# A conditioned transformer block on one core: the opening's loads and steps in another order, and the last token tile finished in two halves

## The chip, the core and the metric

The kernel runs on one core of a Trainium2 chip. The metric is the device time of one execution in microseconds (us), the median of several runs. Engines are named as in the profile: PE is TensorE's matmul side and PEld its weight loads, DVE is VectorE, ACT is ScalarE, POOL is GpSimd, SP is SyncE, which here only issues DMAs. L338 is line 338 of the kernel before.

## The reference, cut to what matters

One sequence of S = 2048 tokens with D = 576 features, 32 heads of 18, and a hidden width of 4608, all in bfloat16:

```
sa, ca, ga, sb, cb, gb = split(silu(c) @ w_mod, 6)        # six rows of 576
h  = layernorm(x) * (1 + ca) + sa
q, k, v = split(h @ wqkv)                                 # 32 heads of 18
logits[s, w] = q[s] . k[s - 2*w] * 18**-0.5,  w = 0..7    # a window of 8 keys, every second token
o  = sum over w of softmax(logits)[s, w] * v[s - 2*w]
x  = x + ga * (o @ wo)
h  = layernorm(x) * (1 + cb) + sb
out = x + gb * (((h @ w_gate) * (h @ w_up)) @ w_down)
```

Keys before the first token are masked with -1e9.

## The kernel before, in words

**Tiles.** Attention goes by chunks of 256 tokens, each two tiles of 128 (index j is the tile in the chunk). 576 features are five tiles of the contraction (kt), the last of 64 rows. The gated part goes by five groups of token tiles, GROUPS (L40): 2, 4, 4, 3 and 3 tiles. Each group has a gate stage (gate_up, L613 to L662) and a down stage (down, L675 to L718). The gate stage runs over 36 slices of 128 hidden columns, and for each makes a gate bank pg and an up bank pu in PSUM (L621), which ACT casts to u_sb and g_sb (L645, L646) and DVE multiplies into hh (L650). The gate and up weights come in nine blocks of four slices (512 columns, two DMAs of 512 KB on SP's queue, L149), the down weights in nine blocks of 576 KB on POOL's queue (L164).

**Order.** The program order of every engine is written out by hand (L63), and each engine works through its own list in that order. Inside the stages of gate and down, pieces of the attention of later chunks are spread evenly between the matmuls (spread, L603; the tables gbg and dbg, L893 and L914). Before the first gate stage there is an **opening** (L729 to L881) which does the whole attention of chunk 0 and the query, key and value products of chunks 1 and 2. Its steps, in the order of before:

- LayerNorm of chunk 0, tile by tile (ln_parts, L225), the transposes of the result (transposed, L263, whose eviction applies the modulation) into hT, and the first modulation columns (mod_columns, L278, from weights wmA).
- a_qj (L353): the products pq = wqk x hT of chunk 0 (L338), 15 matmuls for a group of up to four 128-column tiles and one token tile, six calls, 90 matmuls; a_ln(1) on DVE stands ahead of them.
- pj (L758): DVE products of queries with keys shifted by the window offset w. lj (L763): PE sums them per head into the bank lgj (L769), the mask first (L767). max_j and sum_j are the softmax (L772, L781).
- a_v (L359): values, PE products pv and pvr (L364, L366), ACT casts to v_sb (L368, L369), POOL DMA to a DRAM tile vd. For chunk 0 the cast stays on the chip as o_sb.
- a_norm, a_t and a_q (L311, L325, L348): the same LayerNorm, transposes and query and key products for chunks 1 and 2, in whole chunks.
- to_keys (L475): PE shifts the softmax weights to the key rows (pk), ACT casts them (keyed). av_mul (L492): DVE weights the values (vsh). av_sum (L499): PE shifts and sums them into three banks po of their own pool, pop, and ACT copies these to oT (L510 to L512).
- mod_row (L290): the row ga as a broadcast. b_wj (L514): the output product pwj (L521), two halves of 288 columns in banks of the common pool; DVE adds to x (L527, L528) and takes the statistics of the second LayerNorm.
- transposed again, to h2T, the input of the first gate stage.
- b_ld (L377): a POOL DMA of 1152 KB that gathers the shifted values of one tile of chunk 1 from vd into vsh. The helper behind (L788) makes this DMA wait until a given weight DMA has landed.

**Queues.** Everything that SP issues is one DMA queue in the order of the text: x of chunk 0, wmA (two pairs of 576 and 72 KB), x of chunk 1 (288 KB), wv (576 and 72 KB), wqk in three pairs (576 and 72, 64 and 8, 512 and 64 KB, L195 to L197), then x of chunk 2, wmB, wo, the weights of mod_row, the residual rows, and the first five blocks of gate and up weights (L804).

**PSUM.** There are eight banks. In the opening five belong to psp0 (all products) and three to pop (po). At the end of the opening both pools are closed and one pool psp of eight banks is opened (L88, L882 to L884).

**The end.** The last group holds three token tiles. Its down stage keeps a bank acc of 512 columns for each tile and one bank accr with the last 64 columns of all (L680, L681). After the first 32 hidden slices, the last four are done by tile: accr of all three, then acc of each (L702 to L711). DVE multiplies by gb (L707, L712) and, after all three tiles have been multiplied, adds to x (L715, L716); SP stores each tile in one DMA (L717).

Of the kernel before, what the change touches and what calls it, by code (L numbers as in the profile page):

```python
# [8 lines left out]
F32 = mybir.dt.float32  # L9
ALU = mybir.AluOpType  # L10
# [8 lines left out]
P = 128  # L19
# [24 lines left out]
def kernel(  # L44
# [40 lines left out]
    wdp = pool("wdp", 3)  # L85
    gup = pool("gup", 3)
    outr = pool("outr", 1)
    guards = [tc.tile_pool(name="psp0", bufs=5, space=PSUM), tc.tile_pool(name="pop", bufs=3, space=PSUM)]  # L88
    psp, pop = [g.__enter__() for g in guards]

    def ps(shape, dt, name):
        return psp.tile(shape, dt, name=name, tag="bank")

    def js(j):
        return slice(j * P, (j + 1) * P)
# [34 lines left out]
    def load_x(i):  # L130
        if i < NCH:
            x_in[i] = sp.tile([P, ST, D], BF, name="x_t1") if i == 1 else xin.tile([P, ST, D], BF, name="x_t")
            nc.sync.dma_start(x_in[i][:], x_rows(i))
# [32 lines left out]
    def load_k(dst, wsrc, c0, n):  # L166
        r = nc.sync.dma_start(dst(slice(0, P), slice(0, KF)), wsrc[0:KF * P, c0:c0 + n].rearrange("(k p) n -> p k n", p=P))
        nc.sync.dma_start(dst(slice(0, 64), KF), wsrc[KF * P:D, c0:c0 + n])
        return r
# [20 lines left out]
    nc.gpsimd.memset(wmCr[64:, :], 0.0)  # L190
    load_wm(wmA, 0, 0)
    load_wm(wmA, 1, 1)
    load_x(1)
    load_k(lambda p, k: wv[p, k, :], A_wqkv, 2 * D, D)
    load_k(lambda p, k: wqk[p, k, 0:D], A_wqkv, 0, D)  # L195
    load_k(lambda p, k: wqk[p, k, D:DP], A_wqkv, 2 * D - 64, 64)
    load_k(lambda p, k: wqk[p, k, DP:2 * D], A_wqkv, D, D - 64)  # L197


    nc.gpsimd.memset(ident[:], 0.0)  # L200
# [105 lines left out]
    def a_ln(i):  # L306
        x = x_in.pop(i)
        xn, rsq, norm = layernorm(lambda j: x[:, j, :], "a")
        aa[i] = dict(xn=xn, rsq=rsq, norm=norm)

    def a_norm(i):  # L311
        aa[i]["rsq"]()
        aa[i]["norm"]()
# [11 lines left out]
    def a_t(i, on_dve=True):  # L325
        a_tiles(i)
        hT = aa[i]["hT"]
        transposed(aa[i]["xn"], lambda m: hT[:, m, :], (0, 1), 0)(on_dve)
# [19 lines left out]
    def a_q(i, g):  # L348
        qk_tiles(i, QGRP[g], slice(0, CH), nc.scalar.copy)
        if g == 2:  # L350
            a_halo(i)

    def a_qj(j, g, evict):  # L353
        qk_tiles(0, QGRPJ[g], js(j), evict)
# [4 lines left out]
    def a_v(i, j):  # L359
        hT = aa[i]["hT"]  # L360
        pv = ps([P, VA * DH], F32, "pv")
        pvr = ps([P, VR * DH], F32, "pvr")
        for kt in range(KT):
            nc.tensor.matmul(pv[:], lhsT=hT[:, kt, js(j)], rhs=wv[:, kt, 0:VA * DH], start=(kt == 0), stop=(kt == KT - 1))  # L364
        for kt in range(KT):
            nc.tensor.matmul(pvr[:], lhsT=hT[:, kt, js(j)], rhs=wv[:, kt, VA * DH:D], start=(kt == 0), stop=(kt == KT - 1))  # L366
        v_sb = vstage.tile([P, DH, H], BF, name="v_sb")[:] if i else v0(j)
        nc.scalar.copy(v_sb[:, :, 0:VA], pv[:].rearrange("p (h d) -> p d h", d=DH))  # L368
        nc.scalar.copy(v_sb[:, :, VA:H], pvr[:].rearrange("p (h d) -> p d h", d=DH))  # L369
        r0 = HALO + i * CH + j * P  # L370
        if i == 0:
            if j == 1:
                nc.gpsimd.dma_start(vd[r0 + P - HALO:r0 + P, :], o_sbs[0][P - HALO:P, j, 0:D])
            return
        nc.gpsimd.dma_start(vd[r0:r0 + P, :], v_sb.rearrange("p d h -> p (d h)"))
# [299 lines left out]
    def down(gi, hh, bg):  # L675
        t0, t1 = GROUPS[gi]
        nj = t1 - t0
        last = FT - FB
        at = spread([(1.0, p) for p in bg], last)
        acc = [ps([P, 512], F32, "acc") for _ in range(nj)]  # L680
        accr = ps([P, 2 * ST, 64], F32, "accr")  # L681

        def mm_a(f, j):
            wb = wd_blk[gi * NBLK + f // FB]
            nc.tensor.matmul(acc[j][:], lhsT=hh[:, f, js(j)], rhs=wb[:, f % FB, 0:512],  # L685
                             start=(f == 0), stop=(f == FT - 1))

        def mm_r(f, j):
            wb = wd_blk[gi * NBLK + f // FB]
            nc.tensor.matmul(accr[:, j, :], lhsT=hh[:, f, js(j)], rhs=wb[:, f % FB, 512:D],  # L690
                             start=(f == 0 and j == 0), stop=(f == FT - 1), skip_group_check=True)

        for f in range(last):
            for j in range(nj):
                mm_a(f, j)
                mm_r(f, j)
            if f % FB == FB - 1:
                load_wd(gi * NBLK + f // FB + 3)
            for piece in at[f]:
                piece()  # L700
        xs = [x1[t // ST][t % ST] for t in range(t0, t1)]
        for j in range(nj):  # L702
            for f in range(last, FT):
                mm_r(f, j)
        o_ts = [gup.tile([P, 512], BF, name="o_t", tag="g_sb" if j % 2 else "u_sb") for j in range(nj)]
        t_r = outr.tile([P, 2 * ST, 64], BF, name="t_r")
        nc.vector.tensor_tensor(t_r[:, 0:nj, :], accr[:, 0:nj, :],  # L707
                                gb_bc[:, None, 512:D].to_broadcast([P, nj, 64]), ALU.mult)
        for j in range(nj):
            for f in range(last, FT):  # L710
                mm_a(f, j)  # L711
            nc.vector.tensor_tensor(o_ts[j][:], acc[j][:], gb_bc[:, 0:512], ALU.mult)  # L712
        for j in range(nj):
            r0 = (t0 + j) * P
            nc.vector.tensor_tensor(xs[j][:, 0:512], o_ts[j][:], xs[j][:, 0:512], ALU.add)  # L715
            nc.vector.tensor_tensor(xs[j][:, 512:D], t_r[:, j, :], xs[j][:, 512:D], ALU.add)  # L716
            nc.sync.dma_start(out_flat[r0:r0 + P, :], xs[j][:])  # L717
        load_wd(gi * NBLK + NBLK + 2)  # L718
# [28 lines left out]
    mod_columns(wmA, 0)  # L747
    for e in ev:
        e()
    a_ln(1)  # L750
    for j in range(ST):
        for g in range(3):
            a_qj(j, g, nc.scalar.copy)

    prods, lgs = {}, {}
    dd0 = smp.tile([P, ST, W, H], F32, name="dd")
# [1 line left out]
    def pj(j, w):  # L758
        off = HALO - DIL * (W - 1 - w) + j * P
        prods[j, w] = prodp.tile([P, KT, P], BF, name="prodj", tag="prod")  # L760
        nc.vector.tensor_tensor(prods[j, w][:], aa[0]["qT"][:, :, js(j)], aa[0]["kT"][:, :, off:off + P], ALU.mult)

    def lj(j, w):  # L763
        if w == 0:
            lgs[j] = ps([P, W, H], F32, "lgj")
            if j == 0:
                nc.tensor.matmul(lgs[j][:], lhsT=ident[:], rhs=maskneg[:], start=True, stop=False, skip_group_check=True)  # L767
        for m in range(KT):
            nc.tensor.matmul(lgs[j][:, w, :], lhsT=prods[j, w][:, m, :], rhs=ind[:, m, :],  # L769
                             start=(m == 0 and j == 1), stop=(m == KT - 1), skip_group_check=True)  # L770
# [17 lines left out]
    def behind(dma, load):  # L788
        tc.add_manual_dep(dma.ins, load.ins.name, SYNC, reason="value rows go first")
# [14 lines left out]
    for g in range(5):  # L804
        load_wgu(g)

    for w in range(2):
        pj(0, w)
    a_norm(1)
    for w in range(2, 4):  # L810
        pj(0, w)
    for w in range(4):
        lj(0, w)
        pj(0, w + 4)
    a_v(0, 0)
    for w in range(4, 8):
        lj(0, w)
    a_v(0, 1)
    for w in range(2):
        pj(1, w)  # L820
    max_j(0)
    for w in range(2, 4):
        pj(1, w)
    a_t(1, False)
    for w in range(4):
        lj(1, w)
    for w in range(4, 6):
# [1 line left out]
    sum_j(0)  # L829
    for w in range(6, 8):  # L830
        pj(1, w)
    a_q(1, 0)
    a_q(1, 1)
    for w in range(4, 8):
        lj(1, w)
    max_j(1)
    mod_columns(wmB, 1)
    a_q(1, 2)
    sum_j(1)
    a_q(1, 3)  # L840
    for j in range(ST):
        to_keys(j)
    av_mul(0, 0)
    a_q(1, 4)
    a_v(1, 0)
    av_mul(0, 1)
    av_sum(0, 0)
    a_v(1, 1)
    a_ln(2)
    aa[2]["rsq"]()  # L850
    av_sum(0, 1)
    av_mul(1, 0)
    aa[2]["norm"]()
    mod_row(lambda p, k: wmC[p, k, :] if k < KF else wmCr[p, :], ga_bc, sc_bc)
    x1_half = b_wj(0)
    av_sum(1, 0)
    av_mul(1, 1)
    a_t(2, False)
    xn2, stat2, rsq2, norm2 = ln_parts(lambda j: x1[0][j], "b")
    x1_half(stat2)  # L860
    rsq2(slice(0, 1))
    av_sum(1, 1)
    a_q(2, 0)
    x1_half = b_wj(1)
    behind(b_ld(1, 0), wgu_in[0])
    behind(b_ld(1, 1), wgu_in[1])
    x1_half(stat2)
    rsq2(slice(1, 2))
    norm2(0)
    ht, _ = h2_of(0)  # L870
    a_q(2, 1)
    transposed(xn2, lambda m: ht[:, m, js(0)], (0,), 2)()
    norm2(1)
    a_q(2, 2)
    a_q(2, 3)
    transposed(xn2, lambda m: ht[:, m, js(1)], (1,), 2)()
    a_q(2, 4)
    for j in range(ST):
        a_v(2, j)
    load_res(1)  # L880
    load_x(4)  # L881
    for guard in [sp_guard] + guards[::-1]:  # L882
# [73 lines left out]
```

## Time and profile before

| What | Value |
|---|---|
| Runs | 575.89 us median (574.8, 575.89, 576.01) |
| The profiled execution | 575.69 us, of which its span is 573.7 us; mean granted clock 0.995 |
| PE busy | 547.6 us, 95% of the span, 5959 matmuls |
| PEld busy | 321.0 us, 56% |
| DVE busy | 327.1 us, 57%, 787 instructions |
| ACT busy | 250.9 us, 44%, 576 instructions |
| POOL busy | 67.2 us, 12%, 103 instructions |
| DMA | 108.13 MB, 188 GB/s on average |
| First matmul of the first gate stage | 63.06 us from the span's start |

A row of a group reads: line, engine, operation, output and inputs by the program's names, shape and number; behind the bar the busy time and the mean of one in ns; then the engine's idle time just before, and what ended it. A row of waits reads: engine, what it ran next, what it waited for, and then the sum in us, the number of times and the longest. A row of the timeline reads: start and busy time in us, engine, line, operation, and in brackets the idle time before it and its releaser. A row of windows reads: the stretch, its length, then busy time and number of instructions of PE, PEld, DVE, ACT and POOL, then the granted clock of PE (1.00 is full), the share of the DMA engines and what they moved in GB/s.

### The profile page before, as it was taken

To read this page: it belongs to the slowest core of one execution; us is meant where nothing else is said; L and a number is where in the kernel's file an instruction comes from. 1 tells how busy PE (TensorE), PEld (TensorE's weight loads), DVE (VectorE), ACT (ScalarE), POOL (GpSimd) and SP (SyncE) were. 2 spreads that over 40 slices of the span, in tenths; PEclk is the share of its full clock that TensorE was granted. 3 is DMA by queue.
4 is the path that set the end of the run, shared out by engine and by line. 5 is a ranking of instruction groups with operands and counts; after the bars stand their busy time and mean duration, and the time that the engine had idled before them with its cause. 6 is when DMAs were issued, how large, how long until landed. Compare 5 with 4: busy or idle time off the path is not lost.

```text
span 573.7 us, 14145 instructions
## 1 busy us (share of the span) xinstructions
PE 547.6 (95%) x5959; PEld 321.0 (56%) x5959; DVE 327.1 (57%) x787; ACT 250.9 (44%) x576; POOL 67.2 (12%) x103
## 2 busy tenths in 40 slices
PE   1897999999999999999999999999999999999996
PEld 1676888566444445656444444565556555565553
DVE  5477679896667787343667777505727614322202
ACT  2354666444455555233255565131366611455500
POOL 7001300222100100131100000122000022000020
PEclk9899999999999999999999999999999999999999
DMA  9999596958444665364433874338646665665063
GB/s 255 279 272 363 169 285 207 345 160 277 129 146 135 223 218 174 119 207 146 145 112 110 264 237 147 97 92 294 192 149 176 211 200 167 186 187 183 1 173 106
DMA packets 72303, 108.13 MB, mean 188 GB/s; under 512 B 4752, under 2 KB 62176, under 8 KB 72112
## 3 DMA queue, kind: packets, MB, share of 16 engines
q1 hardware_dynamic: 60464, 61.42, 35.3%
q0 software_dynamic: 11168, 45.81, 25.5%
q8 instruction: 46, 0.75, 0.6%
q14 instruction: 17, 0.14, 0.1%
q10 hardware_dynamic: 608, 0.00, 0.1%
HBM read 102.78 MB, written 4.44 MB: 187 GB/s over the span
## 4 chain that ended last, share of the span: by engine, by line
PE 82%; issue 3%; DMA 3%; DVE 0%; POOL 0%; ACT 0%; SPq 0%; POOLq 0%; DVEq 0%
PE pg L621 25%; PE acc L685 21%; PE pu L621 20%; PE pq L338 4%; PE accr L690 3%; PE pw L538 2%; PE pv L364 2%; PE lg L399 1%; DMA wd<-in_B_w_down_dram 1%; DMA wgu<-in_B_w_up_dram 1%; PE tr_pA L270 1%; PE oT_pA L469 0%; PE tr_pB L270 0%; PE pwr L536 0%; POOL vsh L383 0%
## 5 line engine op out<-in xcount | busy, mean ns | idle before, releaser
L621 PE MATMUL pg<-h2T,wgu 64*128 64x512 bf16 (+2 forms) x1440 | 277.3, 333 | 0.0
L621 PE MATMUL pu<-h2T,wgu 64*128 64x512 bf16 (+2 forms) x1440 | 276.0, 333 | 0.0
L621 PEld LDWEIGHTS <-wgu 64*128 64x128 bf16 x2880 | 141.4, 94 | 107.1 <-issue 0.5
L685 PE MATMUL acc<-wd,hh 128*128 128x512 bf16 x576 | 149.4, 380 | 0.5 <-DMA wd<-in_B_w_down_dram 0.4
L645 ACT CAST u_sb<-pu 128x512 bf16<-128x512 f32 (+2 forms) x180 | 90.1, 501 | 136.5 <-PE pg L621 133.1
L650 DVE TENSOR_TENSOR hh<-g_sb,u_sb 128x512 bf16<-128x512 bf16 (+2 forms) x180 | 66.2, 369 | 102.6 <-ACT g_sb L646 97.8
L690 PE MATMUL accr<-wd,hh 128*128 128x64 bf16 x576 | 101.0, 193 | 0.0
L646 ACT CAST g_sb<-pg 128x512 bf16<-128x512 f32 (+2 forms) x180 | 91.4, 508 | 0.0
L685 PEld LDWEIGHTS <-hh 128*128 128x128 bf16 x576 | 56.0, 98 | 62.7 <-issue 1.7
L164 POOL DMA_DIRECT2D wd<-in_B_w_down_dram x45 | 33.8, 752 | 282.7 <-PE accr L690 230.0
L621 PE MATMUL pg<-h2T,wgr 64*128 64x512 bf16 (+2 forms) x180 | 60.2, 335 | 0.6 <-ACT v_sb L369 0.6
L621 PE MATMUL pu<-h2T,wgr 64*128 64x512 bf16 (+2 forms) x180 | 60.2, 335 | 0.3 <-ACT u_sb L645 0.3
L690 PEld LDWEIGHTS <-hh 128*128 128x128 bf16 x576 | 52.4, 98 | 2.9 <-issue 0.9
L338 PE MATMUL pq<-hT,wqk 128*128 128x256 bf16 (+1 forms) x405 | 46.7, 268 | 5.0 <-DMA wqk<-in_A_wqkv_dram 4.3
L389 DVE TENSOR_TENSOR prod<-qT,kT 128x1280 bf16<-128x1280 bf16 x56 | 44.7, 818 | 2.8 <-PE lg L399 2.8
L338 PEld LDWEIGHTS <-wqk 128*128 128x128 bf16 x405 | 35.6, 102 | 11.4 <-DMA wqk<-in_A_wqkv_dram 4.3
L449 DVE TENSOR_TENSOR vsh<-vsh,attn 128x1152 bf16<-128x1152 bf16 x56 | 40.9, 750 | 0.0
L259 DVE TENSOR_SCALAR h2T<-tr_pA,modc 128x256 bf16<-128x256 bf16 (+1 forms) x30 | 9.7, 377 | 36.8 <-PE tr_pA L270 36.8
L383 POOL DMA_DIRECT2D vsh<-vd x14 | 12.6, 901 | 140.7 <-DVE o_sb L460 88.0
L621 PEld LDWEIGHTS <-wgr 64*128 64x128 bf16 x360 | 18.1, 94 | 17.3 <-issue 4.8
L341 ACT CAST qT<-pq 128x512 bf16<-128x512 f32 x16 | 9.3, 582 | 34.9 <-PE pq L338 34.9
L364 PE MATMUL pv<-wv,hT 128*128 128x504 bf16 x80 | 20.9, 395 | 0.0
(149 smaller groups left out, 435.6 us busy)
## 6 DMA issues: line engine op xcount, KB each, us to landing
wd<-in_B_w_down_dram POOLq DMA_DIRECT2D x45, 576.0 KB, 4.6
wgu<-in_B_w_gate_dram SPq DMA_DIRECT2D x45, 512.0 KB, 4.0
wgu<-in_B_w_up_dram SPq DMA_DIRECT2D x45, 512.0 KB, 5.2
vsh<-vd POOLq DMA_DIRECT2D x14, 1152.0 KB, 7.3
x_r<-in_A_x_dram SPq DMA_DIRECT2D x8, 288.0 KB, 6.3
out_dram<-x SPq DMA_DIRECT2D x16, 144.0 KB, 4.3
x_t<-in_A_x_dram SPq DMA_DIRECT2D x7, 288.0 KB, 6.3
vd<-v_sb POOLq DMA_DIRECT2D x14, 144.0 KB, 2.9
```

The lines of the kernel that those rows point to most:

```text
L164: return nc.gpsimd.dma_start(wb[:], B_w_down[r0:r0 + FB * P, :].rearrange("(k p) n -> p k n", p=P))
L338: nc.tensor.matmul(pq[:, gi, :], lhsT=wqk[:, kt, m * P:(m + 1) * P], rhs=hT[:, kt, cols], start=(kt == 0), stop=(kt == KT - 1))
L364: nc.tensor.matmul(pv[:], lhsT=hT[:, kt, js(j)], rhs=wv[:, kt, 0:VA * DH], start=(kt == 0), stop=(kt == KT - 1))
L383: return nc.gpsimd.dma_start(vsh[:].rearrange("p w d h -> p w (d h)"), vsrc)
L389: nc.vector.tensor_tensor(prod[:], aa[i]["qT"][:], aa[i]["kT"][:, :, off:off + CH], ALU.mult)
L449: nc.vector.tensor_tensor(v, v, at, ALU.mult)
L621: return nc.tensor.matmul(bank[:, 0:N], lhsT=lhs, rhs=rhs, start=first, stop=last, skip_group_check=True)
L645: nc.scalar.copy(u[:, 0:N], pu[:, 0:N])
L646: nc.scalar.copy(g[:, 0:N], pg[:, 0:N])
L650: nc.vector.tensor_tensor(hh[:, f, 0:N], gu[0][:, 0:N], gu[1][:, 0:N], ALU.mult)
L685: nc.tensor.matmul(acc[j][:], lhsT=hh[:, f, js(j)], rhs=wb[:, f % FB, 0:512], start=(f == 0), stop=(f == FT - 1))
L690: nc.tensor.matmul(accr[:, j, :], lhsT=hh[:, f, js(j)], rhs=wb[:, f % FB, 512:D], start=(f == 0 and j == 0), stop=(f == FT - 1), skip_grou ...
```

## The change

Two regions change.

**The opening.** The pools of PSUM are opened in another order. The three pairs of wqk loads go ahead of x of chunk 1 and wv. The six a_qj calls go in another order (the second tile's first group second) and ahead of a_ln(1); the rsq step of chunk 1 (two ACT instructions) comes right behind a_ln(1). Between there and the first gate stage the same steps are interleaved differently: the values of chunk 0 come behind the first products pj and ahead of the lj, the transposes and query products of chunk 1 are spread among the lj, the values of chunk 1 and the transposes of chunk 2 and mod_row come ahead of to_keys, the query products of chunk 2 are put between the av_sum. The two b_ld of chunk 1 go from the middle of b_wj(1) to the end of the opening, behind the DMAs that write the values of chunk 2 on POOL's queue, and they wait for the fourth and fifth weight block (wgu_in[3] and [4]) where they waited for the first two. No step is added or left out.

**The end.** In the last group, the third token tile is summed in two banks of 256 columns, for all 36 hidden slices: two matmuls of 256 columns where one of 512 was, 36 more in all. The additions of the last 64 columns (DVE) come first for all tiles; then each tile, and for the last tile each half, is summed, multiplied, added and stored before the next one's instructions. The additions of the first two tiles (128x512) are on GpSimd, those of the halves on DVE. There are four stores (576, 576, 256 and 320 columns) where there were three.

The diff, with context lines cut:

```
-    guards = [tc.tile_pool(name="psp0", bufs=5, space=PSUM), tc.tile_pool(name="pop", bufs=3, space=PSUM)]
-    psp, pop = [g.__enter__() for g in guards]
+    guards = [tc.tile_pool(name="pop", bufs=3, space=PSUM), tc.tile_pool(name="psp0", bufs=5, space=PSUM)]
+    pop, psp = [g.__enter__() for g in guards]
...
-    load_x(1)
-    load_k(lambda p, k: wv[p, k, :], A_wqkv, 2 * D, D)
     load_k(lambda p, k: wqk[p, k, 0:D], A_wqkv, 0, D)
     load_k(lambda p, k: wqk[p, k, D:DP], A_wqkv, 2 * D - 64, 64)
     load_k(lambda p, k: wqk[p, k, DP:2 * D], A_wqkv, D, D - 64)
+    load_x(1)
+    load_k(lambda p, k: wv[p, k, :], A_wqkv, 2 * D, D)
...
+        final = gi == NG - 1
+        acc = [ps([P, 512], F32, "acc") for _ in range(nj - final)]
+        halves = [(ps([P, CH], F32, "acc"), slice(CH * h, CH * (h + 1))) for h in range(2)] if final else []
...
+            for a, cs in [(acc[j], slice(0, 512))] if j < len(acc) else halves:
+                nc.tensor.matmul(a[:], lhsT=hh[:, f, js(j)], rhs=wb[:, f % FB, cs], start=(f == 0), stop=(f == FT - 1))
...
+        if final:
+            for j in range(nj):
+                nc.vector.tensor_tensor(xs[j][:, 512:D], t_r[:, j, :], xs[j][:, 512:D], ALU.add)
+            for j in range(nj):
+                r0 = (t0 + j) * P
+                for a, cs in [(acc[j], slice(0, 512))] if j < nj - 1 else halves:
+                    for f in range(last, FT):
+                        wb = wd_blk[gi * NBLK + f // FB]
+                        nc.tensor.matmul(a[:], lhsT=hh[:, f, js(j)], rhs=wb[:, f % FB, cs], start=False, stop=(f == FT - 1))
+                    nc.vector.tensor_tensor(o_ts[j][:, cs], a[:], gb_bc[:, cs], ALU.mult)
+                    adder = nc.gpsimd if j < nj - 1 else nc.vector
+                    adder.tensor_tensor(xs[j][:, cs], o_ts[j][:, cs], xs[j][:, cs], ALU.add)
+                    stored = slice(0, CH) if cs.stop == CH else slice(cs.start, D)
+                    nc.sync.dma_start(out_flat[r0:r0 + P, stored], xs[j][:, stored])
+            return
...
+    for j, g in ((0, 0), (1, 0), (0, 1), (0, 2), (1, 1), (1, 2)):
+        a_qj(j, g, nc.scalar.copy)
     a_ln(1)
-    for j in range(ST):
-        for g in range(3):
-            a_qj(j, g, nc.scalar.copy)
+    aa[1]["rsq"]()
```

The opening's order behind that point, as it stands after the change:

```
    for w in range(3):
        pj(0, w)
    aa[1]["norm"]()
    for j in range(ST):
        a_v(0, j)
    for w in range(3, 6):
        pj(0, w)
    a_t(1, False)
    for w in range(4):
        lj(0, w)
    for w in range(6, 8):
        pj(0, w)
    a_q(1, 0)
    for w in range(4, 8):
        lj(0, w)
    for w in range(4):
        pj(1, w)
    max_j(0)
    a_q(1, 1)
    a_q(1, 2)
    for w in range(4):
        lj(1, w)
    for w in range(4, 6):
        pj(1, w)
    sum_j(0)
    for w in range(6, 8):
        pj(1, w)
    a_q(1, 3)
    for w in range(4, 8):
        lj(1, w)
    a_ln(2)
    aa[2]["rsq"]()
    max_j(1)
    a_q(1, 4)
    mod_columns(wmB, 1)
    aa[2]["norm"]()
    sum_j(1)
    for j in range(ST):
        a_v(1, j)
    a_t(2, False)
    mod_row(lambda p, k: wmC[p, k, :] if k < KF else wmCr[p, :], ga_bc, sc_bc)
    for j in range(ST):
        to_keys(j)
    av_mul(0, 0)
    av_mul(0, 1)
    a_q(2, 0)
    av_sum(0, 0)
    av_mul(1, 0)
    a_q(2, 1)
    av_sum(0, 1)
    av_mul(1, 1)
    xn2, stat2, rsq2, norm2 = ln_parts(lambda j: x1[0][j], "b")
    ht, _ = h2_of(0)
    av_sum(1, 0)
    x1_half = b_wj(0)
    x1_half(stat2)
    rsq2(slice(0, 1))
    a_q(2, 2)
    av_sum(1, 1)
    norm2(0)
    a_q(2, 3)
    x1_half = b_wj(1)
    x1_half(stat2)
    rsq2(slice(1, 2))
    transposed(xn2, lambda m: ht[:, m, js(0)], (0,), 2)()
    norm2(1)
    a_q(2, 4)
    for j in range(ST):
        a_v(2, j)
    transposed(xn2, lambda m: ht[:, m, js(1)], (1,), 2)()
    behind(b_ld(1, 0), wgu_in[3])
    behind(b_ld(1, 1), wgu_in[4])
```

## What the change will do: the prediction

> **What bounds the kernel now.** I read the page's busy times first, then PE's waits by stretch, then the windows, the DMA issues and the timeline of the end.
>
> ```profile
> span 573.7 us, 14145 instructions
> PE   1897999999999999999999999999999999999996
> PEclk9899999999999999999999999999999999999999
> ```
>
> PE is full from the fifth slice on. What can be won lies in the first four slices (57 us) and in the last. Two answers on PE's waits say where: between 10 and 30 us, and between 18 us and the start of the first gate stage.
>
> ```profile
> PE pq L338 <- DMA wqk<-in_A_wqkv_dram: 4.3, 1, 4.3
> ...
> PE lgj L769 <- DVE prodj L761: 2.4, 1, 2.4
> PE pwj L521 <- ACT oT L510: 1.9, 1, 1.9
> PE tr_pA L270 <- DVE ln_xn L243: 1.4, 1, 1.4
> PE pq L338 <- ACT hT L261: 0.7, 3, 0.3
> PE pg L621 <- ACT v_sb L369: 0.6, 1, 0.6
> PE pk L484 <- DVE attn L785: 0.4, 1, 0.4
> ```
>
> 4.3 us before the first product of chunk 0, then six waits of 7.4 us together (2.4 + 1.9 + 1.4 + 0.7 + 0.6 + 0.4). From 63.06 us, where the first gate matmul starts, to 574 PE's waits are only some 1.8 us. So the gate and down stages run at PE's rate, and an opening that ends earlier moves everything behind it by as much. The windows show a third loss (columns: stretch, length, busy PE, PEld, DVE, ACT, POOL, clock, DMA share, GB/s):
>
> ```profile
> 18.00:21.70 3.70, 3.69 (x70) 3.58 (x67) 0.89 (x2) 2.02 (x5) 0.00 (x0) 1.00 1.09 266
> 21.70:24.07 2.37, 0.01 (x1) 0.01 (x1) 1.64 (x6) 0.66 (x3) 0.00 (x0) 1.00 1.09 205
> 24.07:28.30 4.23, 4.12 (x43) 2.26 (x44) 3.50 (x9) 0.70 (x2) 0.00 (x0) 0.60 1.14 294
> ```
>
> Behind the 2.37 us in which PE waits for DVE's products the granted clock is 0.60; in the records it is half from 24.87 to 28.28 us (3.41 us), which costs half of that, 1.7 us.
>
> **Part 1, the loads: -2.95 us.** SP's queue delivers in order. In the issues of 3.9 to 10.6 us x of chunk 1 lands at 10.31, wv at 12.2 and 12.4, wqk's first pair at 14.40 and 14.76; pq starts at 14.45. Between the last of wmA (9.5) and wqk's first DMA (14.4), 288 + 648 + 576 KB came, 0.3 MB per us. Moved past, x of chunk 1 and wv (936 KB) are worth about 2.95 us: wqk's first pair lands at some 11.5, the others by 14.1, x of chunk 1 at 14.9, wv at 16.8 to 17.0. PE has hT from ACT and DVE between 11.2 and 12.4, so pq can start at 11.5. Who pays: a_ln(1) (DVE, 1.9 us) now has x only at 14.9, behind pq's start, with nothing on PE waiting before a_t(1); wv is wanted by a_v(0,0) when pq ends (14.45 to 21.34 before, now 11.5 to some 18.2), 1.2 us behind its landing. Were the order worth nothing, the term is 0; if pq starts at once at full clock it is up to 1.8 more: of its 90 matmuls the 34 between 14 and 18 us go at 107 ns and the rest at 53.
>
> **Part 2, the hole and the slow clock: -1.7 us, and pauses of 5.2 instead of 7.4: -2.2 us.** I walked the new order with the old durations. After pq PE now has a_v(0) and a_t(1) while DVE makes prodj (0.445 us each) and normalizes chunk 1; the 2.37 us hole goes, and with it the stretch at half clock. What is late next, each from the rows of the same operation:
>
> - a_q(1,0) behind ACT's hT: the three waits stand as before, 0.7.
> - lgj of the second tile: DVE has max_j(0) (0.42 + 0.42), sum_j(0) (0.58 + 0.35 + 0.42) and four prodj (1.8) in front of its last half, 4.0 us, PE 20 lgj and 10 pq of a_q(1,3) at 0.03 and 0.109, 1.7; DVE comes some 1.6 ahead: 0.7.
> - av_sum(0,0): keyed on ACT, then vsh (1.3 us for a half) on DVE, and PE has only a_q(2,0) as cover, 10 x 0.109 = 1.1: 0.85.
> - av_sum(1,0) behind DVE's vsh: 0.3.
> - b_wj(1) behind ACT's oT: ACT has rsq and the kT cast of a_q(2,3) in its queue, and PE only 1.1 us of pq as cover: 1.2 (the same wait was 1.9).
> - a_v(2,1) wants a bank that DVE still reads (pwj): 0.35.
> - first gate matmul: the last transposes' evictions stand on ACT behind the casts of a_v(2,1): 1.1 (before 0.6).
>
> Sum 5.2. The transposes' wait (1.4) is covered by a_q(2,3) and b_wj(1); to_keys (0.4) by a_v(1), a_t(2) and mod_row. Bounds: 7.4, if each cover fails by as much as before (0), and 4.0 with the two largest halved (-3.4). No instruction is added here, so no engine has more work; of the 16 us from 47 to 63 PE is busy 12.1, DVE 10.0 and ACT 9.1, so that DVE and ACT have room to be ahead of PE, but not much. The swap of pools costs nothing on an engine; it changes which bank is free first.
>
> [...]
>
> **Part 3, b_ld later: 0.** Both gathers (1152 KB each, issued 47.34 and 49.79, landed 56.8 and 60.5 before) now move during the first gate stage. They are first read (L449) 24.4 us behind its start, so they themselves are in time. What they can push is wgu block 5: issued 67.75 and landed 77.2 and 78.65 before, first used 85.45, 6.8 us of slack. From the gate's start to that landing the queues must bring 2.36 MB of vsh, 0.66 of wm5, 1.18 of wd and 1.05 of wgu, 5.25 MB; at the 0.30 to 0.35 MB per us that full stretches of before show (308 and 351 GB/s from 67 to 75) this is 15 to 17.5 us plus some 1 of latency, against 22.4. If the gathers' small rows went at half that, PE would wait some 4 us.
>
> **Part 4, the end: +0.15 us.** The timeline of before (start, busy time):
>
> ```profile
> 566.48 0.69 DVE L712 TENSOR_TENSOR o_t<-acc,gb_bc 128x512 bf16<-128x512 f32 x1 [0.51 <-PE acc L685]
> ...
> 568.81 0.41 DVE L715 TENSOR_TENSOR x<-o_t,x 128x512 bf16<-128x512 bf16 x1
> ...
> 569.35 1.53 SPq L717 DMA_DIRECT2D out_dram<-x  x3
> ```
>
> The three stores are issued at 569.35, 570.05 and 570.51; the last lands at 572.65. After: 36 matmuls of 512 columns become 72 of 256, 2 x 0.109 for 0.2155, +0.09; accr's bank is the fifth now, freed by ACT 0.15 later; so the first multiplication is at 566.72. Then the adds of tiles 0 and 1 go one behind the other on POOL, each of length P, and SP issues the halves' stores behind tile 1's, 0.46 apart: last issue = 566.72 + 0.69 + 0.12 + 2P + 0.92 = 568.45 + 2P, but not ahead of 569.72, where DVE's halves (0.36 + 0.22 each) end. No row shows a two-input operation on POOL. Below, DVE's row for it, 0.415: 569.72, 0.79 sooner. Above, POOL's copy of 128x640 takes 0.717, 1.12 ns a column; twice that for two inputs, 1.15 for 512: 570.75, 0.24 later. I take 1.15, since the row is POOL's own; the last store is smaller (80 for 144 KB), about -0.1. Net +0.15; break-even with before at P = 1.03.
>
> [...]
>
> **Sum.** -2.95 - 1.7 - 2.2 + 0.15 = -6.7. 575.69 - 6.7 = **569.0 us**. The profiled execution is 0.2 below the median of the runs, which adds nothing to the sum. 0.2% (1.15 us) is about what a measurement of this kernel can tell from no change.
>
> **Rivals.**
>
> - **Clock, better:** pq runs at full clock from its first matmul, since PE has stood only 1.3 us instead of 4.26: 569.0 - 1.8 = 567.2. Against: DVE's prodj waits for ACT's casts of the products, and wv lands at 17.0, which gives part of it back.
> - **Clock, worse:** one of the new pauses (1.2 and 1.1 are the largest) falls so that the clock is halved again for 3.41 us: 569.0 + 1.7 = 570.7.
> - **The loads don't do what they say:** wqk is not served sooner, as the DMAs are full anyway (share 1.0 and more from 4 to 18 us): 569.0 + 2.95 = 572.0. Against: the landings of before follow the order of issue.
> - **A new wait in the first gate stage:** the gathers hold back wgu block 5 (part 3): 569.0 + 4 = 573.0. It decides from a rate below 5.25 / 22.4 = 0.23 MB per us.
> - **First call on POOL, no change:** the adds are the first two-input operations on POOL; if the first of an operation is held up by L, the last store goes back by L and the time is 569.0 + L, within 0.2% of before for L from 5.5 to 7.8. In this trace POOL's first copy (0.716 at 10.02) and its second (0.717) take the same, and its first select starts 0.1 behind the memset ahead of it, so nothing of the kind is seen. [...]
> - **Slower:** the two adds on POOL stand in series ahead of the last two stores on SP's queue, so each us of P counts twice. From P = (6.85 + 2.06) / 2 = 4.5 us the end eats the opening's gain, from 5.0 the kernel is slower by 0.2%; at 6 us (eight times the copy's row) 568.45 + 12 = 580.45 is 9.9 behind 570.51, less 6.85: 578.8 us. Nothing in the rows is near 5 us on POOL.
>
> **How the numbers follow.** Forecast, 569.0 with 567.8 to 570.4 from the bounds of the pauses and of P: 0.70. Clock better 0.08, clock worse 0.08, loads 0.03, gate stage 0.05, POOL's first call 0.03, slower 0.03. The range 566.5 to 572.2 holds the first four and some of the gate stage, the outer ends of the pauses' bounds (566.9 and 571.2) too. Faster: 0.94; same 0.03; slower 0.03.
>
> **What would show it.** pq's first matmul at 11.5 and its wait down from 4.3 to 1.3; the wait for prodj gone from the top of the list and no slice of PEclk below 9 between 18 and 56 us; the first gate matmul at 56.2 to 56.6 instead of 63.06; no wait of PE on wgu above 0.5 in the stage behind it; POOL's two rows at 1.15 and the last store issued 0.2 later against the last accr matmul. Wrong would be a gate start above 58.5 (covers fail), a wait on wgu, or POOL rows of several us.

## The result and the profile after

| | before | after |
|---|---|---|
| Runs, median | 575.89 us (574.23 to 576.01) | 568.76 us (567.81 to 569.60) |
| Ratio, 95% interval | | 0.9881 [0.9861, 0.9901] |
| Profiled execution, its span | 575.69, 573.7 us | 569.60, 567.7 us |
| pq (queries and keys of chunk 0) starts, and ends | 14.45, 21.34 | 11.79, 19.67 |
| First gate matmul (below: the gate start) | 63.06 | 57.39 |
| From it to the first acc matmul of the last four slices | 502.35 | 502.50 |
| From there to the end of the span | 8.29 | 7.81 |

The forecast was 569.0 us. The profiled execution of after is the slowest of its five; the walk from stage to stage below is made on it and adds up to 6.0 us, where the medians differ by 7.1. The rows of pq and of the gate start, before and after:

```profile
14.45 6.89 PE L338 MATMUL pq<-hT,wqk 128*128 128x128 bf16 x90 [4.26 <-DMA wqk<-in_A_wqkv_dram]
63.06 0.27 PE L621 MATMUL pg<-h2T,wgr 64*128 64x256 bf16 x1 [0.63 <-ACT v_sb L369]
```

```profile
11.79 7.88 PE L338 MATMUL pq<-hT,wqk 128*128 128x128 bf16 x90 [1.54 <-DMA wqk<-in_A_wqkv_dram]
57.39 0.27 PE L621 MATMUL pg<-h2T,wgr 64*128 64x256 bf16 x1 [1.16 <-ACT h2T L261]
```

The page of after:

```profile
span 567.7 us, 14223 instructions
...
PE   3998999999999999999999999999999999999996
...
PEclk9999999999999999999999999999999999999999
```

The dip in the second slice of the clock (14 to 29 us) is gone. PE's waits between 10 and 30 us begin with the loads, and between 18 us and the first gate matmul they are these (sum, times, longest):

```profile
PE pq L338 <- DMA wqk<-in_A_wqkv_dram: 1.5, 1, 1.5
...
PE pg L621 <- ACT h2T L261: 1.2, 1, 1.2
PE pwj L521 <- ACT oT L510: 1.1, 1, 1.1
PE po L507 <- DVE vsh L496: 0.8, 1, 0.8
PE lgj L786 <- DVE prodj L778: 0.5, 1, 0.5
PE pq L338 <- ACT hT L261: 0.4, 2, 0.2
PE pv L364 <- DVE h2T L259: 0.3, 1, 0.3
PE po L507 <- ACT oT L510: 0.3, 1, 0.3
```

The wait for wqk fell from 4.3 to 1.5 us, the seven others sum to 4.6 where six summed to 7.4. Behind the first gate matmul nothing waits on wgu. The end of after (start, busy time, in brackets the idle time before):

```profile
561.74 2.26 POOL L722 TENSOR_TENSOR x<-o_t,x 128x512 bf16<-128x512 bf16 x2 [7.08 <-DVE o_t L720]
561.82 1.02 DVE L720 TENSOR_TENSOR o_t<-acc,gb_bc 128x512 bf16<-128x512 f32 x2 [0.17 <-PE acc L719]
562.88 1.27 DVE L722 TENSOR_TENSOR x<-o_t,x 128x256 bf16<-128x256 bf16 x1
562.92 2.52 SPq L724 DMA_DIRECT2D out_dram<-x  x4
564.07 0.41 DVE L720 TENSOR_TENSOR o_t<-acc,gb_bc 128x256 bf16<-128x256 f32 x1
564.52 0.29 DVE L722 TENSOR_TENSOR x<-o_t,x 128x256 bf16<-128x256 bf16 x1
```

The two adds on POOL took 1.15 and 1.14 us, 2.26 from the start of the first to the end of the second. What no step of the prediction had is the third row: DVE's add of 128x256 stands for 1.27 us, until just behind the end of POOL's second add; its twin in the last row takes 0.29.

The profile also records when the clock changes. Full clock is granted at 18.04 us in before and at 17.35 in after. Ahead of that pq's matmuls go at 107 ns, behind it at 56 (the prediction read 53): of its 90, the first 34 in before and the first 52 in after. So pq took 7.88 instead of 6.89. Below, the stretch ahead of the grant is called the cold start, and a stretch of 3.41 us at half clock behind it a spell.

The mean granted clock of every run is on record as well. A spell lowers it by 0.003, and the end of the span, where the clock falls once more (0.50 from 571.00 us in before, from 566.90 in after), by at most 0.003 in the profiled executions. In the five runs of after it is 0.998 or 0.999, so none has a spell; in 63 of the 74 runs of the kernel before that stand beside the experiments below it is 0.996 or less, so these have at least one.

### The profile page after: what moved, and what is told of

The parts are those of the page before. It is cut to its first block, busy times and chain, and to the rows that moved or that the text cites. A ratio compares the mean times of both kernels' runs of the same rounds, so it can differ in the third digit from the quotient of the medians.

```text
span 567.7 us, 14223 instructions
## 1 busy us (share of the span) xinstructions
PE 547.7 (96%) x5995; PEld 325.1 (57%) x5995; DVE 327.9 (58%) x787; ACT 250.4 (44%) x576; POOL 69.5 (12%) x105
## 4 chain that ended last, share of the span: by engine, by line
PE 55%; issue 31%; DMA 6%; POOL 3%; DVE 2%; ACT 2%; SPq 1%; POOLq 0%
PE pg L621 15%; PE pu L621 12%; PE acc L688 11%; PE pq L338 6%; PE pv L364 2%; POOL wd L164 2%; DMA wd<-in_B_w_down_dram 2%; DMA wgu<-in_B_w_up_dram 2%; PE accr L692 2%; PE pw L538 2%; DMA wqk<-in_A_wqkv_dram 1%; PE lg L399 1%; PE po L507 1%; DMA vd<-v_sb 1%; PE tr_pA L270 1%
## 5 line engine op out<-in xcount | busy, mean ns | idle before, releaser
L688 PE MATMUL acc<-wd,hh 128*128 128x512 bf16 (+1 forms) x596 | 146.9, 368 | 0.4 <-DMA wd<-in_B_w_down_dram 0.3
L456 DVE TENSOR_TENSOR vsh<-vsh 128x1152 bf16<-128x1152 bf16 x28 | 20.5, 751 | 0.0
```

Source lines behind the costliest of these rows:

```text
L456: nc.vector.tensor_tensor(vsh[:, d], vsh[:, d], vsh[:, 4 + 2 * s:6 + 2 * s], ALU.add)
L688: nc.tensor.matmul(a[:], lhsT=hh[:, f, js(j)], rhs=wb[:, f % FB, cs], start=(f == 0), stop=(f == FT - 1))
```

## The experiments

Theory: the gain is the earlier loads and the shorter waits of PE in the opening, plus a spell at half clock that goes; the end is worth nearly nothing. Rivals: the loads alone, the clock alone, the end, or the place of the gathers. A spell or a cold start differs from run to run (the mean clock of the runs of the kernel before goes from 0.991 to 1.0), so what one profiled execution shows of it need not be the median. Each kernel's time stands beside runs of the kernel before on the same chip, whose medians went from 574.99 to 576.05; so ratios are given.

**The loads alone, and all but the loads.** The kernel before with this edit, and the changed kernel with its reverse:

```
-    load_x(1)
-    load_k(lambda p, k: wv[p, k, :], A_wqkv, 2 * D, D)
     load_k(lambda p, k: wqk[p, k, 0:D], A_wqkv, 0, D)
...
+    load_x(1)
+    load_k(lambda p, k: wv[p, k, :], A_wqkv, 2 * D, D)
```

> The kernel before with the order of the loads alone changed (wqk ahead of x of chunk 1 and wv), nothing else. Theory (the loads and the new order add up): pq starts at some 11.8 us instead of 14.45, 2.65 sooner; a_ln(1) still stands ahead of the products prodj on DVE and now waits for x of chunk 1 until 14.9, which pq hides. The 2.4 us hole and the half clock behind it stay. Gate start 60.0 to 61.0, time 1.7 to 2.9 us below the kernel before. Rival 1 (the DMAs are full, so the order brings nothing): pq starts at 14.4, time within 0.5 us of before. Rival 2 (the gain is given back in the old order, because wv or x of chunk 1 is then late for a_v(0) or for the transposes of chunk 1): pq early, but gate start above 62.5.

> The changed kernel with the loads in the order of before. Theory (terms add up): pq starts at 14.4 instead of 11.8, 2.6 later, and everything behind it follows: gate start near 59 to 60, time 1.7 to 2.9 us above the changed kernel, that is 4.2 to 5.5 below the kernel before. Rival (the new order hangs on the early loads, and without them falls back to holes): less than 2 us below the kernel before.

The loads alone: 572.94 us, ratio 0.9952 [0.9934, 0.9969], 2.9 below before; pq at 11.08, gate start 60.31. All but the loads: 572.16, 0.9935 [0.9914, 0.9957], 3.7 below. PE's waits in all but the loads, between 18 us and the gate start, are those of after, wait by wait (4.6). With the loads alone they are those of before but for the transposes' 1.4 (5.7 instead of 7.4): this execution has a second spell, from 50.49 to 53.91 us, just ahead of them, and from pq's end to the gate start it takes 41.54 us where before took 41.72, so nothing was won by it. 2.9 + 3.7 = 6.6 of 7.1: the two parts add up within the noise, and no rival of these runs stands. All but the loads was expected 4.2 to 5.5 below before and came out at 3.7: in the new order of steps the loads are worth 3.1 us by the ratios and 3.4 by the medians, where 1.7 to 2.9 was expected, though the noise covers the difference.

**The hole filled.** The kernel before, with matmuls that nothing reads where PE stood:

```
+    warm = pop.tile([P, 2, CH], F32, name="po")
+
+    def fill(n):
+        for _ in range(n):
+            nc.tensor.matmul(warm[:, 0, 0:P], lhsT=ident[:], rhs=ident[:], start=True, stop=True)
...
+    fill(36)
     for w in range(4):
         lj(0, w)
```

> The kernel before with 36 more matmuls (128x128 by 128 columns of ident, into a bank that nothing reads) between pq and the first lgj, where PE waits 2.4 us for the products of DVE. They do no work for the result; they only keep PE busy for 36 x 56 ns = 2.0 us. Theory (the hole is what halves the clock from 24.87 to 28.28): the clock stays full there, gate start 1.2 to 1.7 us sooner, time 1 to 1.7 below before. Rival 1 (the half clock hurts nobody, since PE there waits for DVE's products anyway): clock full, time within 0.5 of before. Rival 2 (the clock falls for another reason): clock 0.5 for some 3.4 us as before, time the same.

574.28 us, 0.9972 [0.9960, 0.9983]: 1.6 below before, without any of the kernel's own work moved. Windows of this kernel, in the columns of the prediction's:

```profile
20.60:22.80 2.20, 2.20 (x43) 2.19 (x41) 0.91 (x4) 0.99 (x3) 0.00 (x0) 1.00 1.08 192
22.80:28.30 5.50, 4.96 (x92) 3.53 (x90) 5.47 (x16) 1.94 (x6) 0.24 (x1) 1.00 1.12 298
```

The clock, 0.60 there before, is 1.00. The half clock did cost what the prediction charged for it. But in this execution there is another spell from 51.27 to 54.68 us, behind the wait for oT, and the mean clock of the runs says the same: 0.996 in the median of the filled kernel, 0.994 in the median of before beside it, that is one spell less and often still one left.

**The values moved alone.** The kernel before, with a_v(0,0) and a_v(0,1) ahead of the first lgj:

```
+    for j in range(ST):
+        a_v(0, j)
     for w in range(4):
         lj(0, w)
         pj(0, w + 4)
-    a_v(0, 0)
     for w in range(4, 8):
         lj(0, w)
-    a_v(0, 1)
```

> The kernel before with one step of the new order alone: the values of chunk 0 (a_v(0,0) and a_v(0,1), 2.6 us of PE) ahead of the first lgj, where PE waits 2.4 us for DVE. Theory 1 (the hole is what costs, and any work of PE fills it): hole and half clock gone, 2.4 to 4 us below before. Theory 2 (the hole comes from ACT and DVE: DVE waits 2.05 us for ACT's rstd behind the casts of pq, and then makes eight products; filled on PE, the wait shows again at the later lgj or at the transposes of chunk 1): 0.5 to 2 below before, what the half clock cost, with a new wait of PE on prodj or ln_xn of 1 us or more.

576.08 us, 0.9999 [0.9986, 1.0012]: nothing, less than either theory. PE's waits from 18 us to its gate start look much better:

```profile
PE pwj L521 <- ACT oT L510: 1.9, 1, 1.9
PE lgj L769 <- DVE prodj L761: 0.9, 1, 0.9
PE pg L621 <- ACT v_sb L369: 0.6, 1, 0.6
PE pk L484 <- DVE attn L785: 0.4, 1, 0.4
PE tr_pA L270 <- DVE ln_xn L243: 0.2, 1, 0.2
PE pq L338 <- ACT hT L261: 0.2, 1, 0.2
```

4.2 us instead of 7.4, and no gain. Part of it only left this view: 40 lgj matmuls ran from 25.07 to 27.70, 66 ns each where ten unhindered ones take some 26, so DVE's products paced them by 1.6 us in waits too short to be listed. In this execution the clock took the rest, in two spells; all twelve runs have a mean clock of 0.991 to 0.993 (before beside them 0.995 in the median):

```profile
30.80:34.20 3.40, 3.39 (x17) 2.33 (x17) 2.47 (x6) 0.59 (x1) 0.00 (x0) 0.50 1.01 219
54.70:58.10 3.40, 3.20 (x19) 2.10 (x18) 2.84 (x10) 0.86 (x3) 0.00 (x0) 0.50 0.83 290
```

**The first half of the new order.** The kernel before, with the new order from prodj to the softmax only (values and a_t(1) ahead of the lgj, the query products of chunk 1 between them); from to_keys on it is the old one:

```
+    for j in range(ST):
+        a_v(0, j)
+    for w in range(3, 6):
         pj(0, w)
+    a_t(1, False)
     for w in range(4):
         lj(0, w)
...
+    a_q(1, 0)
     for w in range(4, 8):
         lj(0, w)
```

> The kernel before, its loads, pools and end untouched, with the new order only from the products prodj to the softmax of chunk 0 (values and transposes of chunk 1 ahead of the lgj, the query products of chunk 1 between them); from to_keys on the old order. The values alone at that place gave nothing, since DVE's eight products then pace the lgj. Theory (with a_t(1) and a_q(1,0) there as well PE has 4.2 us of work while DVE makes its products, so PE's hole goes): 2 to 3.5 us below before, PE's waits from 18 us to the gate start from 7.4 down to 5 or less. Rival (the hole was not on the path, and what the new order brought, 3.7 us, comes from its second half, the waits of pwj 1.9 and tr_pA 1.4): within 1 us of before, the wait for prodj small and others larger.

575.05 us, 0.9980 [0.9968, 0.9993]: 0.7 below before, nearer to the rival. So of the 3.7 us that the whole order is worth, the larger part needs the second half (by difference; it was not run alone). Part of that is the clock: five of the twelve runs have a mean of 0.989 or 0.990, below every run of before beside them (0.991 to 1.0). The waits that stand in this kernel are the ones that the second half takes away:

```profile
PE pwj L521 <- ACT oT L510: 1.9, 1, 1.9
PE lgj L769 <- DVE prodj L761: 1.5, 1, 1.5
PE tr_pA L270 <- DVE ln_xn L243: 1.4, 1, 1.4
```

**PE kept busy, in both kernels.** The changed kernel with 44 such fills ahead of the first transposes, 10 between the halves of mod_columns and 26 behind it; the kernel before with 44, 10, 72, and 36 in the hole:

```
...
+    fill(44)
     ev = [transposed(xn0, lambda m, j=j: hT0[:, m, js(j)], (j,), 0) for j in range(ST)]
-    mod_columns(wmA, 0)
+    mod_columns(wmA, 0, lambda: fill(10))
+    fill(26)
```

> The changed kernel with 80 more matmuls (128 columns of ident, into a bank that nothing reads) where PE has nothing to do in the first 12 us: 44 ahead of the first transposes, 10 between the two halves of mod_columns, 26 behind it. They do no work for the result. Theory (pq runs at half clock because PE has been idle before it, and the boundary of a 3.41 us window that comes after it decides when the full clock is granted): the clock is full before pq starts, the 90 matmuls of pq take 5.0 us at 56 ns instead of 7.9, pq ends at 16.8 to 17.2, gate start 55 to 56, time 1.3 to 2.5 us below the changed kernel's 568.8, and the times of the runs lie closer together than 1.8 us. Rival 1 (the 107 ns of the first pq matmuls come from loads or DMA traffic, not the clock): pq as long as before, time the same. Rival 2 (pq shorter, but wv at 17 us and DVE's products take it back): pq short, a new wait of PE behind it, time within 0.5 of the changed kernel.

> The kernel before with matmuls that do no work for the result wherever PE stood in the first 24 us: 44 ahead of the first transposes, 10 between the halves of mod_columns, 72 behind it, 36 between pq and the first lgj. So the clock is full in all of it, and what is left between this kernel and the changed one with PE kept busy (567.46) is what the change takes from PE's waits themselves. Theory (clock and waits add up): pq takes 5.0 to 5.4 us instead of 6.9, no half clock at 25 us; time 571.5 to 573, that is 2 to 3.5 below before, and 4 to 5.5 above the changed kernel with PE kept busy, which is the loads (2.7) and the pauses (2 to 2.8). Rival 1 (nearly all of the change is clock): less than 3 above it. Rival 2 (DVE and ACT, not PE, set the opening's end, so the clock gives nothing here): within 1 us of before.

After with PE kept busy: 567.46 us, 0.9861 [0.9844, 0.9879]; the kernel before so: 574.36, 0.9977 [0.9968, 0.9987]. In the profiled executions full clock is granted at 5.83 and at 8.16 us and stays until the end of the work. pq in the two, the changed kernel first:

```profile
11.34 5.42 PE L340 MATMUL pq<-hT,wqk 128*128 128x128 bf16 x90
17.12 1.24 PE L366 MATMUL pv<-wv,hT 128*128 128x504 bf16 x5 [0.36 <-DMA wv<-in_A_wqkv_dram]
```

```profile
14.33 1.56 PE L340 MATMUL pq<-hT,wqk 128*128 128x128 bf16 x25
16.83 3.88 PE L340 MATMUL pq<-hT,wqk 128*128 128x128 bf16 x65 [0.94 <-DMA wqk<-in_A_wqkv_dram]
```

The changed kernel behaves as the theory had it. Its gain over after is 1.3 us by the medians and 0.20% by the ratios, whose intervals overlap. The kernel before gains less than the theory said (1.7 by the medians, 1.3 by the ratio, not 2 to 3.5), no more than with the hole alone filled: at full clock pq overtakes its loads and waits 0.94 us for a later piece of wqk. Four of its eleven runs still have a spell (mean clock 0.994 or 0.995). With the clock nearly out of both, the change is worth 0.9977 - 0.9861 = 1.16%, 6.7 us, where the theory had 4 to 5.5. In the profiled executions pq ends 3.95 us sooner (it starts 3.00 sooner and the wait for the later piece goes), from there to the gate start it is 2.0 shorter, and 0.7 is left for the stages and the end. Rival 1 (the change is mostly clock) falls.

**The end.** First the kernel before with the new end only; then the changed kernel with all adds on DVE; then with each add on POOL done twice, the first time into a tile that nothing reads:

```
-                    adder = nc.gpsimd if j < nj - 1 else nc.vector
+                    adder = nc.vector
```

```
...
+                    if j < nj - 1:
+                        nc.gpsimd.tensor_tensor(spare[:, 0:2, :].rearrange("p a b -> p (a b)"), o_ts[j][:, cs], xs[j][:, cs], ALU.add)
                     adder.tensor_tensor(xs[j][:, cs], o_ts[j][:, cs], xs[j][:, cs], ALU.add)
```

> The kernel before with the change of the last group alone (two banks of 256 columns, tiles added and stored one by one, two adds on GpSimd). Theory from the trace of the changed kernel: the stages pay 0.1 to 0.2 us for the 36 matmuls, the end from the first acc matmul of the last four slices to the end of the span is 7.8 instead of 8.3 us; together -0.2 to -0.5, below what the times can tell. The prediction had +0.15. Rival (the separate placement of stores and the GpSimd adds cost): the end longer than 8.3.

> The changed kernel with the two adds of 128x512 in the last group on DVE instead of GpSimd. Theory (two adds of 1.15 us one behind the other on GpSimd set the last two stores, and DVE's add of 128x256 stands 1.27 us while GpSimd adds): the add of the first half takes 0.2 to 0.3 us, the last store is issued 0.5 to 0.6 us sooner against the first acc matmul of the last four slices (4.5 to 4.6 behind it instead of 5.13), time 0 to 0.8 below the changed kernel, which the times alone can hardly tell. Rival 1 (SP's issues, 0.46 to 0.55 apart, set the end): at most 0.2 sooner. Rival 2 (DVE becomes the bound of the end): no sooner or later.

> The changed kernel with each of the two GpSimd adds of the last group done twice, the first time into a tile that nothing reads. Theory (the two adds stand one behind the other ahead of the last two stores, so each us of an add counts twice): the two extra adds of 1.15 us put the last store 2.2 to 2.4 us later against the first acc matmul of the last slices (7.4 instead of 5.13), time 2.0 to 2.6 above the changed kernel's 568.8. DVE's add of 128x256 stands until GpSimd is done, over 2 us. Rival (GpSimd adds are hidden behind DVE and SP): less than 1 us.

| | time, ratio to before | from DVE's multiplication of the last 64 columns (t_r) to the last store's issue |
|---|---|---|
| before | 575.89 | 4.90 us |
| new end only | 576.20, 1.0003 [0.9990, 1.0015] | 4.95 |
| after | 568.76, 0.9881 [0.9861, 0.9901] | 4.92 |
| adds on DVE | 568.76, 0.9888 [0.9870, 0.9905] | 4.42 |
| adds on POOL doubled | 571.62, 0.9925 [0.9909, 0.9941] | 7.42 |

The new end is no change that the times can tell. With the adds on DVE the last store goes out 0.5 us sooner, as the theory had it; the time does not show it, and the profiled execution of that kernel, the slowest of its six, holds a wait of 2.2 us for the down weights wd at 393 us that after's did not. Without POOL's adds both halves are added in 0.29 us:

```profile
564.62 0.29 DVE L722 TENSOR_TENSOR x<-o_t,x 128x256 bf16<-128x256 bf16 x1
565.28 0.29 DVE L722 TENSOR_TENSOR x<-o_t,x 128x256 bf16<-128x256 bf16 x1
```

Doubling two adds of 1.15 cost 2.5 us on the last store and 0.44% (2.5 us) in time: POOL's adds do stand in series ahead of it. The row of the store is the firmer of the two, since this execution also waits 1.9 us for wd in a down stage, which after's did not, and what the medians owe to that is not known. In the doubled kernel, too, DVE's add of the second half takes longer (0.79) and that of the first, which starts between two adds of POOL, does not (0.29):

```profile
561.53 1.15 POOL L724 TENSOR_TENSOR prod<-o_t,x 128x512 bf16<-128x512 bf16 x1 [6.87 <-DVE o_t L721]
562.68 0.29 DVE L725 TENSOR_TENSOR x<-o_t,x 128x256 bf16<-128x256 bf16 x1
562.77 1.21 POOL L725 TENSOR_TENSOR x<-o_t,x 128x512 bf16<-128x512 bf16 x1
562.89 0.42 DVE L721 TENSOR_TENSOR o_t<-acc,gb_bc 128x256 bf16<-128x256 f32 x1
563.34 0.79 DVE L725 TENSOR_TENSOR x<-o_t,x 128x256 bf16<-128x256 bf16 x1
```

**The gathers put back, and the best of it.** The changed kernel with b_ld of chunk 1 in b_wj(1) again, behind wgu_in[0] and [1]; and the changed kernel with PE kept busy and all adds on DVE:

> The changed kernel with the two gathers of chunk 1 where they were before (in b_wj(1), behind the first two weight blocks). Theory of the prediction (they cost nothing at either place): gate start and time within 0.5 us of the changed kernel, no wait of PE on weights in the first gate stage in either. Rival 1 (they were moved because they hold up PE or the casts at the end of the opening): gate start 1 us later or more. Rival 2 (at their new place they do cost something in the first gate stage): the stretch from the first gate matmul to the first acc matmul of the last slices, 502.5 us, gets shorter by over 0.3.

> Both together: the 80 matmuls that keep PE busy, and the adds of the end on DVE. Theory (both are real and independent): 1.8 to 3.1 us below the changed kernel's 568.8, that is 565.7 to 567.0. Rival: one of them gives nothing, and the time is that of the other alone.

Gathers back: 568.22 us, 0.9875 [0.9857, 0.9892], gate start 56.20, 502.42 us from there to the last slices. The place costs nothing either way. Best: 566.61 us (566.26 to 567.48), 0.9851 [0.9834, 0.9869]; on the same chip the changed kernel with the gathers back ran 568.22 and with the adds on DVE 568.76. So it is some 1.6 to 2.1 us below the change, within the theory's 565.7 to 567.0, though the interval of its ratio still overlaps that of the change. Against PE kept busy alone (567.46, 0.9861) it is 0.9 lower, which these intervals can't tell from nothing: that the two gains add is not shown.

## Why the prediction was right

**Sum and sign.** 569.0 was forecast, 568.76 measured. The terms, on the profiled executions:

- *Loads, -2.95.* -2.66 at pq's start (wqk landed 0.3 later than the rate gave), -2.9 by the kernel with the loads alone. Right.
- *What the prediction took as given: pq takes as long as before.* It does on average, not in one execution: 7.88 for 6.89 here. Over the profiled executions without fills ahead of pq it takes 6.59 to 8.05 us in the six with the old order of the loads and 6.84 to 7.88 in the five with the new one, by where the grant of the clock falls; both have a mean of 7.3. So the 1.0 us that this pair of executions loses there is luck, and without it the walk adds up to 2.66 + 4.0 + 0.33 = 7.0, against 7.1 by the medians. It is also why the gate start came at 57.39, where 56.2 to 56.6 was named as the sign; with the gathers back and a pq of 7.21 it is 56.20.
- *Hole, half clock and pauses, -1.7 - 2.2 = -3.9.* From pq's end to the gate 41.72 us became 37.72: -4.0. The waits fell by 2.8 (to 4.6, where 5.2 was forecast), and no spell at half clock came in this opening. Filling the hole alone showed the 1.6 us of clock in the kernel before, as charged, and the mean clocks show that after has no spell in any of its runs. But the reason given, that the hole goes "and with it the stretch at half clock", is too simple: with the values alone moved the hole went, and the half clock came back at 31 and 55 us. With the whole order no spell came (0.998 or 0.999 in the five runs of after). How the 4.0 us divide between clock and waits can't be told sharply, since a spell can also stand in the place of a wait (of the transposes' 1.4 with the loads alone).
- *The list of what is late next.* All seven came at the instruction that was named, with the forecast in brackets: pg 1.2 (1.1), pwj 1.1 (1.2), av_sum(0,0) 0.8 (0.85), lgj 0.5 (0.7), hT 0.4 (0.7), a_v(2,1) 0.3 (0.35), av_sum(1,0) 0.3 (0.3). In the last two the releaser was another than said: DVE's h2T and ACT's oT.
- *Gathers, 0.* Right; no wait on wgu. No run shows the "1 of latency" of part 3 by itself; the last two stores of after, 64 and 80 KB, landed 1.7 us behind their issue.
- *End, +0.15.* The adds took 1.15 and 1.14, the size taken from the copy's row by doubling it, which was a guess that came out. The last store went out 0.02 later against t_r. But from its issue to the end of the span it is 2.7 us instead of 3.2, where 0.1 was allowed for the smaller store; so the end gave -0.48 and the stages +0.15. The times can't tell any of this from nothing.
- *Small slips in the working.* Of the 1.8 us of waits counted behind the gate start, 0.6 is the wait ahead of the first gate matmul, which the list has already. The 570.4 at the top of the inner range is not what its own bounds give: the pauses alone reach 571.2. Nothing hangs on either.

**Rivals.** "Clock, better" did not come by itself; it had to be made, and then brought some 1.3 us. "Clock, worse" is in none of the seven profiles that have the whole new order; the last section shows how busy PE is in its windows. The loads did what they say. POOL's first add (1.15) was as long as its second (1.14). The rival on the slower side stood on each us of an add counting twice: that was shown, at 1.15 us an add it decides nothing.

## What to carry to other kernels

A hole of PE that is filled with other work can be worth nothing, if a chain on DVE or ACT sets the pace behind it or the clock falls elsewhere: look at the mean pitch of the matmuls that follow, not only at the listed waits (the values moved alone: listed waits of 4.2 us instead of 7.4, the lgj at 66 ns instead of 26, two spells, ratio 0.9999). Loads go in the order of their first use, also where that pushes large ones back, as long as the pushed ones land before PE has done the work that is ahead of them (2.9 us here, with the loads alone). Where PE stands in the first microseconds anyway, matmuls that nothing reads can buy full clock for the first real ones (granted here at 5.83 instead of 17.35 us, 1.3 us by the medians); that pays only as far as their loads have landed (in the kernel before, pq then waited 0.94 us for wqk).

## What the runs showed of the hardware

- **The clock fell without silence.** The changes of the granted clock lie on a grid of 3.413 us whose place differs from run to run: 18.04, 24.87, 28.28 and 571.00 us in before, 17.35 and 566.90 in after. Below, a window is a stretch between two points of this grid. In the kernel before, the window 21.45 to 24.86 had PE busy for 0.93 of 3.41 us and was followed by half clock; windows with 1.50 (the loads alone, the hole filled and the values moved alone) and 1.56 (the loads alone) were too. Windows with 1.71 and 2.09 (the new end alone) and 1.87 (before) were not, and in after no window behind the grant and ahead of the gate has less than 2.25. In the kernel with the new end alone the same 2.4 us hole fell across two windows (busy 2.62 and 1.71), and the clock stayed full. Busy time alone does not part the two kinds: a window with 1.84 us (the first half of the new order, 30.99 to 34.40), most of its matmuls of one column (the second modulation columns), and one with 2.07 us (the values moved alone, 27.40 to 30.81), most of them lgj of 32 columns, were followed by half clock too. What sets these two apart was not shown.
- **The grant of full clock** came at the end of a window that pq had filled by 2.8 us or more, or the added matmuls by 2.75 (the changed kernel with PE kept busy, granted at 5.83); windows that pq filled by 2.15 of 3.41 (10.53 to 13.94 in after) and by 2.53 (13.74 to 17.16 in the kernel with the values moved alone) brought none. So pq ran at half rate, 107 ns a matmul instead of 56, for between 2.8 us (all but the loads) and 5.95 us (the values moved alone). Half of that, 1.4 to 3.0 us, is what it cost where pq did not wait for its loads, by where the grid fell; the fastest and the slowest run of after are 1.8 us apart.
- **DVE's bf16 add of 128x256 took longer beside an add on POOL.** It took 0.29 us without one (both halves with the adds on DVE, the second half in after), 1.27 in after and 0.79 with POOL's adds doubled beside one, and both times it ended 0.15 us behind the end of POOL's add. DVE's multiplications from PSUM beside the same adds took 0.42 (128x256) and 0.69 (128x512); with the adds on DVE they took 0.42 and 0.69 too.
